# A chain of attention, a channel mix and a gated mix on one core: the value weight by seven products

## The chip, the cores and the metric

One core of a Trainium2 chip runs the whole program. The metric is the device time of one execution in microseconds; smaller is better. Engines: PE (TensorE, matmuls), DVE (VectorE), ACT (ScalarE), POOL (GpSimd), SP (SyncE, which here only issues DMAs).

## The reference

Three operations in a row, all in fp32, batch 8, 576 positions. An attention with random features (8 heads of 64) gives x of 512 channels. A first mix and a second mix follow, each batch by itself:

```python
# attention: phi(x) = [exp(p), exp(-p)], p = x @ w_phi less its largest magnitude
num = q_p @ (k_p.T @ v); den = q_p @ k_p.sum(seq) + 1e-6; x = num / den
# first mix, w_k 512x1024, w_v 1024x512, w_r 512x512
xk = mu_k * x + (1 - mu_k) * x_prev;  xr = mu_r * x + (1 - mu_r) * x_prev
x = sigmoid(xr @ w_r) * (relu(xk @ w_k) ** 2 @ w_v)
# second mix, w_val 512x512, conv_w 5x512, w_out 512x512
gate = sigmoid(causal convolution of x with conv_w)
out = (gate * (x @ w_val)) @ w_out
```

## The kernel before

A product of two fp32 matrices is made of three passes: each operand is split into a high half of reduced precision (ACT copies it) and the low rest (DVE subtracts), and high x high, high x low and low x high are added in a PSUM bank. Four of the five weight products (k, r, v, out) moreover go by seven products instead of eight, after Winograd: both matrices are cut into four quarters, seven sums of quarters are multiplied, and the results joined. The fifth, by the value weight, is plain: `gemm`, four column tiles by two halves by twelve matmuls of 128x128 by 128x288, 96 in a round; `split` makes its four high and four low halves in the page `y`.

The program runs in two parts. In the attention (up to some 297 us) PE projects, turns and sums, and beside it the weights are converted from the 64-bit input: `narrow` on ACT and DVE, sums of quarters (`combine`) and halves (`part_two`, `pool_tt`) on POOL and ACT, then to DRAM (`ws`); wk alone stays in SBUF (`wkt`). The second part has rounds `it` = 0 to 8. A round multiplies batch `it` by k (`st_k`), r (`st_r`) and v (`st_v`), and batch `it - 1` by value (`st_val`) and out (`st_out`); DVE and ACT run that batch's convolution (`conv`) beside it. On PE a round has three phases: k alone, then r and value by turns, then v and out by turns. Weight units of 1 MB are fetched by SP (`fetch_unit`) into a ring of three pages u0 to u2 or into a page that is free (xf, dd, ot).

`seven` drives r and out: `combos` yields sums of quarters one after the other, `operand` splits each into a place of the ring `ops`, which has four places for all products together. Results go from banks to SBUF through ACT copies and DVE additions; with `fork`, `begun` copies the first product's bank to a second one so that sums continue in it. Round `it`'s x lies in the page `xx`, loaded by `prep`, which mixes it with its shifted copy (ACT and DVE) into `xf` and `dd`.

The order on each engine is not the order of the code: every step is a task with a due time (`when`, in units of TIME us for a round; T, ODD and FIRST for the attention), and `Order.run` lays the tasks out on the engines by costs written in the file, each engine executing its list in order. Lines the prediction touches: L386 matmul, L960 ACT copies (`acts`), L402 the low halves (`less`), L951 sums (`dve`), L954 multiply-adds (`fma`), L420 loads, L486 and L497 POOL's sums and casts of conversion, L1066 the memset in `prep`, L1103 `begun`.

Of the kernel before, what the change touches and what calls it, by code (L numbers as in the profile page):

```python
# [20 lines left out]
TB = 288  # L21
# [4 lines left out]
def pattern(bits):  # L26
# [9 lines left out]
ODD = dict(q_proj=-0.118, k_proj=-0.204, turn=-0.103, sums=0.978, num=0.197, back=0.009)  # L36
FIRST = dict(q_proj=-5.403, k_proj=-0.991, tails=-2.94, turn=-1.923, sums=-0.992)
FROM, TO = 0, 28.375
# [6 lines left out]
PORT = 0.234  # L45
# [12 lines left out]
SOON, EARLY = 0, 0.332  # L58
SPLIT, FORK_R = 8, False
LIMIT = 1.274  # L60
# [252 lines left out]
def build(ctx, tc, qt, kt, vv, wphi, mu, wk, wr, wv, wval, cw, wout, out):  # L313
# [194 lines left out]
    def combine(quarters, n, emit):  # L508

        (a11, t11), (a12, t12), (a21, t21), (a22, t22) = quarters  # L510
        f = sb("F", [128, 512])
        s1 = (lambda: f[:, 0:n])
        pool_tt(n, s1, a21, a22, ALU.add, [t21, t22], [(f, 0)], new=[f])
        emit(0, a11, [t11])
        if n == 512:
            s3, t3 = a21, t21
            pool_tt(n, s3, a11, a21, ALU.subtract, [t11], [t21])
            s2, t2 = a11, t11
            pool_tt(n, s2, s1, a11, ALU.subtract, [(f, 0)], [t11])
# [11 lines left out]
        emit(6, a22, [t22])  # L531
# [3 lines left out]
    def convert(name, w, group, k, tick):  # L535
# [20 lines left out]
        elif name != "wk" and k == 1:  # L556
            stage = []

            def emit(p, x, r):
                if p % 2 == 0:  # L560
                    stage.append(sb("ql", [128, 2, 2, 256]))
                hl, e, u = stage[-1], p % 2, units[name] + (p if name == "wv" else p // 2)
                at = (lambda h: hl[:, e, h]) if name == "wv" else (lambda h: hl[:, h, e])
                part_two(x, lambda: at(0), lambda: at(1), 256, r, [(hl, e, h) for h in range(2)],
                         new=[] if e else [hl])
                if e or p == 6:
# [11 lines left out]
            combine([((lambda q=q, c=c: q[:, 256 * c:256 * c + 256]), (q, c)) for q, c in  # L578
                     ((got[0], 0), (got[1], 0), (got[0], 1), (got[1], 1))], 256, emit)
# [320 lines left out]
    def moe():  # L900
# [21 lines left out]
        TIME = 79.6  # L922
# [90 lines left out]
        def combos(ops, n, q, tmp, parts, due):  # L1013

            def sub(p, out, x, y):
                due(p, None)
                dve(n, out, x, y, ALU.subtract, tokens(x, y), out.tok)

            def op(p, k):
                for i, x in enumerate(parts(tmp if k is None else q[k])):  # L1020
                    due(p, i)
                    ops[p, i] = operand(x)

            op(0, 0)
            yield
            op(1, 2)
            sub(1.4, tmp, q[3], q[1])
            sub(1.6, q[1], q[1], q[0])
            sub(1.8, q[0], q[3], q[1])
            yield  # L1030
            for p, k in enumerate((0, 1, None, 3, 2), 2):
                op(p, k)
                if p == 2:
                    sub(2.2, q[2], q[2], q[0])
                yield
# [25 lines left out]
        def prep(it):  # L1061
# [3 lines left out]
            if it == 0:  # L1065
                add("POOL", 0.15, lambda: nc.gpsimd.memset(x()[:, :, 0:1], 0.0), r=[("page", "xx")], w=["x0"])  # L1066
# [18 lines left out]

        def split(it, t, c, x, dst):
            when(it, t)
            h, l = (At(dst or ("xx", "dd")[i], 2304 * i * bool(dst) + 576 * c, 576) for i in range(2))
            acts(576, lambda: h(F32R), x, AF.Copy, x.tok, h.tok)
            add("DVE", d_time(576), lambda: less(nc.vector, l(F32R), x(), h(F32R)), r=tokens(x, h), w=l.tok)  # L1090
# [62 lines left out]
        def st_v(it, start):  # L1153
# [7 lines left out]
            for p in range(7):  # L1161
# [3 lines left out]
                u = fetch_unit(it, start(p) - 10, units["wv"] + p, None if p else ("xf", 0))  # L1165
# [41 lines left out]
        def gemm(name, it, start, src, after):  # L1207

            mov = [At(src or ("xx", "dd")[i], 2304 * i * bool(src), 4, 2, 288) for i in range(2)]
            for m in range(4):  # L1210
                if m == 0:
                    when(it, start(0) - 10)
                    renew("xf", F32R)
                if m % 2 == 0:
                    u = fetch_unit(it, start(2 * m) - 10, units[name] + m // 2, None if m else ("xf", 0))
                o = wide()
                for h in range(2):
                    t = start(2 * m + h)
                    when(it, t)
                    add("PE", t_mm(TB, 12), lambda m=m, h=h, o=o, u=u: product(  # L1220
                        o, h, [(unit_at(u, 0, c, m % 2), unit_at(u, 1, c, m % 2)) for c in range(4)],
                        [[a(F32R)[:, c, h] for c in range(4)] for a in mov], True, True),
                        r=tokens(*mov) + u.tok, w=[o], new=[] if h else [o])
                when(it, t - SOONER)
                after(m, o, both(o), t + 1.6)

        def seven(name, it, start, q, tmp, p5, land, lead, places, fork):
# [3 lines left out]
                           lambda p, i: when(it, start(p) - lead if i is not None else start(0) + p - lead - 4))  # L1231
            banks = {}
            for p in range(7):
# [5 lines left out]
                if p == 6 or isinstance(place, tuple):  # L1239
# [4 lines left out]
                for _ in range(1 if p or 0 < it < 7 else 2):  # L1244
                    next(steps, None)
# [30 lines left out]
        def st_r(it, start):  # L1276
            land = {(a, h): x2_pair(it, 2 * a, h) for a in range(2) for h in range(2)}
            q = [At("dd", 576 * i, 2, 288) for i in range(4)]
            for got in seven("wr", it, start, q, At("tmp", 0, 2, 288), At("sp", 1152, 2, 288), land, 10, [None] * 6 + [("ot", 0)],
                             FORK_R and it > 0):  # L1280
                if got is None:
                    continue
                t, a, h, b, r = got
                when(it, t)
                x = land[a, h]
                acts(576, x, b or x, AF.Sigmoid, r, x.tok)
# [25 lines left out]
        def st_out(i, it, start):  # L1312
            land = {(a, h): At("y", 1152 + 1152 * a + 576 * h, 2, 288) for a in range(2) for h in range(2)}
            q = [x2_pair(i, 2 * a, h) for a in range(2) for h in range(2)]
            for got in seven("wout", it, start, q, At("y", 0, 2, 288), At("y", 576, 2, 288), land, 8,
                                       ["dd", ("dd", 1024), ("ot", 0), ("dd", 0), ("dd", 1024), ("ot", 0), None] if it < 7 else [None] * 7, it < 7):
# [12 lines left out]
        for it in range(9):  # L1329
# [3 lines left out]
            if it:  # L1333
                conv(it - 1, it, -10, 1.8)
                when(it, 6 if it < 8 else -30)
                if it == 8:
                    renew("xx", F32R)
                    renew("dd", F32R)
                else:
# [6 lines left out]
            if it < 8:  # L1346
                st_r(it, at(22.3, 3.18))
            if it:
                st_val(it, at(23.9, 3.18))
                if it < 8:  # L1350
                    when(it, 47)
                    renew("y", F32)
            v = st_v(it, at(46.2, 4.77 if 0 < it < 7 else 3.18)) if it < 8 else ()
            o = st_out(it - 1, it, at(49.4, 4.77) if it < 7 else at(68.5 if it == 7 else 49.4, 1.59)) if it else ()
# [109 lines left out]
```

## Time and profile before

| | before |
|---|---|
| median of 3 runs | 941.8 us (937.82 to 941.82) |
| the profiled execution | 946.79 us |
| its span, first to last instruction | 945.0 us |
| PE busy | 911.5 us, 96% |
| DVE, ACT busy | 822.9 us, 719.0 us |
| POOL busy (attention only) | 185.8 us |
| granted PE clock, mean | 0.994 |

The rows come from one profiled execution, so sums are made against its own 946.79 us (945.0 us of span and 1.8 us around it); the median of the runs is 5.0 us lower. Busy is the time in which at least one instruction of the engine is on record. Instructions of ACT and DVE overlap their neighbours a little, so the distance of two starts says what one costs when they follow each other.

### The profile page before, as it was taken

To read this page: it belongs to the slowest core of one execution; us is meant where nothing else is said; L and a number is where in the kernel's file an instruction comes from. 1 tells how busy PE (TensorE), PEld (TensorE's weight loads), DVE (VectorE), ACT (ScalarE), POOL (GpSimd) and SP (SyncE) were. 2 spreads that over 40 slices of the span, in tenths; PEclk is the share of its full clock that TensorE was granted. 3 is DMA by queue.
4 is the path that set the end of the run, shared out by engine and by line. 5 is a ranking of instruction groups with operands and counts; after the bars stand their busy time and mean duration, and the time that the engine had idled before them with its cause. 6 is when DMAs were issued, how large, how long until landed. Compare 5 with 4: busy or idle time off the path is not lost.

```text
span 945.0 us, 28048 instructions
## 1 busy us (share of the span) xinstructions
PE 911.5 (96%) x11696; PEld 895.0 (95%) x11696; DVE 822.9 (87%) x1276; ACT 719.0 (76%) x1435; POOL 185.8 (20%) x322
## 2 busy tenths in 40 slices
PE   7999989998998999999999999999999999999997
PEld 6998988898898999999999999999999999999997
DVE  5999989888877799789979978988997897899695
ACT  4998978888798979479767947966876794787453
POOL 0387975675671000000000000000000000000000
PEclk9999999999999999999999999999999999999999
DMA  6657788888866583777488477658738847764883
GB/s 218 206 196 221 234 265 291 285 264 285 287 223 218 206 283 121 254 271 244 167 298 288 151 268 273 229 223 277 269 113 301 291 154 282 252 196 172 281 308 133
DMA packets 79774, 224.33 MB, mean 237 GB/s; under 512 B 10144, under 2 KB 35104, under 8 KB 66592
## 3 DMA queue, kind: packets, MB, share of 16 engines
q1 hardware_dynamic: 70784, 213.04, 66.3%
q10 hardware_dynamic: 8864, 9.50, 2.8%
q8 instruction: 92, 1.51, 0.7%
q14 instruction: 34, 0.28, 0.1%
HBM read 186.87 MB, written 35.65 MB: 235 GB/s over the span
## 4 chain that ended last, share of the span: by engine, by line
PE 76%; DVE 8%; ACT 6%; DMA 4%; issue 3%; POOL 2%; ACTq 0%; SPq 0%; DVEq 0%; POOLq 0%
PE c L386 59%; PE b L386 15%; PE b L749 2%; DVE ops L402 2%; DMA out<-y 1%; DVE dd L662 1%; DVE x L951 1%; POOL wkt L486 1%; DMA ops<-in_kt 1%; DMA xx<-in_wr 1%; ACT u L718 1%; ACT ops L960 1%; DMA xx<-in_wval 1%; DMA u<-ws 1%; DMA xx<-in_wv 1%
## 5 line engine op out<-in xcount | busy, mean ns | idle before, releaser
L386 PE MATMUL c<-ops,u 128*128 128x288 f32 x1968 | 275.7, 296 | 5.0 <-DVE ops L402 3.4
L386 PEld LDWEIGHTS c<-ops,u 128*128 128x128 f32 x1968 | 266.3, 188 | 7.2 <-DVE ops L402 4.4
L386 PE MATMUL c<-ops,wkt 128*128 128x288 f32 x1344 | 180.2, 295 | 2.3 <-ACT x L399 1.2
L386 PEld LDWEIGHTS c<-ops,wkt 128*128 128x128 f32 x1344 | 178.3, 188 | 3.2 <-ACT x L399 1.3
L662 DVE TENSOR_REDUCE dd<-b 128x4 f32<-128x512 f32 (+1 forms) x144 | 86.5, 622 | 20.8 <-PE b L386 19.6
L954 DVE SCALAR_TENSOR_TENSOR g<-x,cwt,g 128x576 f32<-128x576 f32 x128 | 102.4, 819 | 0.0
L960 ACT ACTIVATE ops<-k 128x576 fp32r<-128x576 f32 x96 | 65.3, 681 | 46.4 <-PE c L386 43.8
L402 DVE TENSOR_TENSOR ops<-k,ops 128x576 fp32r<-128x576 f32 x96 | 71.8, 756 | 26.0 <-ACT ops L960 25.8
L386 PE MATMUL b<-wph,ops 64*128 64x128 f32 x1152 | 88.3, 288 | 6.3 <-DMA ops<-in_kt 4.4
L386 PEld LDWEIGHTS b<-wph,ops 64*128 64x128 f32 x1152 | 77.1, 194 | 9.7 <-ACT u L718 3.2
L386 PE MATMUL b<-g,y 128*64 128x65 f32 x2176 | 74.4, 224 | 5.3 <-issue 3.0
L386 PEld LDWEIGHTS b<-g,y 128*64 128x64 f32 x2176 | 68.9, 139 | 8.2 <-issue 3.6
L767 ACT ACTIVATE y<-b 128x512 f32<-128x512 f32 x128 | 68.5, 627 | 4.2 <-PE b L749 3.2
L960 ACT ACTIVATE sp<-c 128x576 f32<-128x576 f32 x50 | 32.5, 650 | 42.9 <-PE c L386 42.7
L960 ACT ACTIVATE k<-k 128x576 f32<-128x576 f32 x98 | 63.1, 681 | 0.3
L399 ACT ACTIVATE x<-b 128x260 f32<-128x260 f32 (+3 forms) x112 | 40.5, 416 | 11.0 <-PE b L749 5.2
L386 PE MATMUL c<-y,u 128*128 128x288 f32 x336 | 48.0, 294 | 0.0
L386 PE MATMUL c<-y,xf 128*128 128x288 f32 x336 | 46.8, 295 | 0.0
L386 PEld LDWEIGHTS c<-y,u 128*128 128x128 f32 x336 | 45.7, 188 | 0.0
L386 PEld LDWEIGHTS c<-y,xf 128*128 128x128 f32 x336 | 45.3, 188 | 0.0
L960 ACT ACTIVATE k<-c 128x576 f32<-128x576 f32 x64 | 41.3, 646 | 5.1 <-PE c L386 3.9
L960 ACT ACTIVATE ops<-xf 128x576 fp32r<-128x576 f32 x48 | 32.7, 683 | 13.8 <-PE c L386 7.9
(160 smaller groups left out, 1819.3 us busy)
## 6 DMA issues: line engine op xcount, KB each, us to landing
u<-ws SPq DMA_DIRECT2D x86, 1024.0 KB, 5.4
xf<-ws SPq DMA_DIRECT2D x16, 1024.0 KB, 6.0
ws<-dd SPq DMA_DIRECT2D x28, 512.0 KB, 4.8
dd<-ws SPq DMA_DIRECT2D x24, 512.0 KB, 5.8
ot<-ws SPq DMA_DIRECT2D x20, 512.0 KB, 5.7
xs<-x SPq DMA_DIRECT2D x16, 576.0 KB, 4.6
xx<-xs SPq DMA_DIRECT2D x8, 1152.0 KB, 7.5
out<-y ACTq DMA_DIRECT2D x32, 288.0 KB, 5.3
```

What stands on the lines that cost most here:

```text
L386: latest[0] = nc.tensor.matmul(**kw)
L399: act(out=out, in_=x, func=AF.Copy)
L402: eng.tensor_tensor(out=out, in0=x, in1=hi.bitcast(F32), op=ALU.subtract)
L486: nc.gpsimd.tensor_tensor(out=o[:, c], in0=a[:, c], in1=b[:, c], op=op)
L662: add("DVE", t_dve(128 * n), lambda: nc.vector.tensor_reduce(out=m[:, 0:n, 0], in_=b3[:, 0:n], axis=AX.X, op=ALU.max, apply_absolute_value ...
L718: act(out=e[:, c, half], in_=b3[:, c], func=AF.Exp, scale=-1.0 if half else 1.0, bias=m[:, 1 - half, c:c + 1])
L749: latest[0] = nc.tensor.transpose(out=out, in_=x[r], identity=ident[r, r])
L767: add("ACT", t_act(512), lambda y=y, half=half: act(out=e[:, y, half, :], in_=bs[y][:], func=AF.Exp, scale=-1.0 if half else 1.0), r=[bs[y ...
L951: add("DVE", d_time(n), lambda: tt(out=out(), in0=x(), in1=y(), op=op), r=r, w=w)
L954: add("DVE", d_time(n) + 0.06, lambda: stt(out=out(), in0=x(), scalar=scalar(), in1=y(), op0=ALU.mult, op1=ALU.add), r=r, w=w)
L960: act(out=out(), in_=x(), func=func, **more)
```

## The change

The value weight of rounds 1 to 7 goes by seven products as well: `st_val` calls `seven` with `fork`, and its products alternate with those of r, as those of v and out do. Sums of quarters are made from x in `x2` into the page `xx` (argument `into`), the operands go through the ring `ops`, and `split` into `y` disappears; `y` receives weight units. The gate (DVE) multiplies each joined quarter. Because `xx` is now used up to the end of value, x of the next round is loaded after that, and its zero column is set anew by a POOL memset in each round. The last round (`last_val`) multiplies plainly as before, from quarters a11, a12, a22 and a21, so a21 is stored as an eighth unit. The value weight's conversion makes sums of quarters like the others: four units per column group, `ws` grows from 34 to 38. The due times of the attention (T, ODD, FIRST, FROM) and some constants of the order are new; TIME is 78.0 instead of 79.6.

```diff
-T = dict(load_q=-5.614, load_k=-4.036, load_v=-2.112, tails=-1.806, q_proj=-1.855, k_proj=-1.864, turn=-0.024,
-         sums=-1.263, num=0.201, back=1.217, finish=1.434, convert=0.307, ones=-1.742, num_step=0.488, scale=0.715,
-         prep=-0.343)
...
+T = dict(load_q=-5.752, load_k=-3.673, load_v=-2.132, tails=-1.806, q_proj=-1.854, k_proj=-1.864, turn=-0.024,
+         sums=-1.263, num=0.201, back=1.217, finish=2.23, convert=0.226, ones=-2.034, num_step=0.361, scale=0.715,
+         prep=-0.396)
...
-FROM, TO = 0, 28.375
+FROM, TO = 0.892, 28.375
...
-    SEVEN = ("wr", "wout")
-    units = {"wr": 0, "wval": 4, "wv": 6, "wout": 13}
-    ws = dram.tile([128, 34, 4, 256], F32, name="ws")
+    SEVEN = ("wr", "wval", "wout")
+    units = {"wr": 0, "wval": 4, "wv": 8, "wout": 15}
+    ws = dram.tile([128, 38, 4, 256], F32, name="ws")
...
-    def combine(quarters, n, emit):
+    def combine(quarters, n, emit, whole=False):
         (a11, t11), (a12, t12), (a21, t21), (a22, t22) = quarters
+        if whole:
+            emit(6, a22, [t22])
+            emit(7, a21, [t21])
...
-        TIME = 79.6
+        TIME = 78.0
...
-        def combos(ops, n, q, tmp, parts, due):
+        def combos(ops, n, q, tmp, parts, due, into=None):
+            at = into or (q[1], q[0], q[2])
...
-            if it == 0:
-                add("POOL", 0.15, lambda: nc.gpsimd.memset(x()[:, :, 0:1], 0.0), r=[("page", "xx")], w=["x0"])
+            add("POOL", 0.15, lambda: nc.gpsimd.memset(x()[:, :, 0:1], 0.0), r=[("page", "xx")],
+                w=["x0"] + [k for c in range(4) for k in span("xx", 577 * c, 1)])
...
+                if isinstance(place, list):
+                    u = fetch_unit(it, start(p) - 10, units[name] + p // 2, place)
+                elif p == 6 or isinstance(place, tuple):
...
         def st_val(it, start):
-            def after(m, o, b, t):
-                g, y = At("g", 576 * m, 576), x2_at(it - 1, m, 0, 576)
-                dve(576, lambda: halves(y()), lambda: halves(g()), b, ALU.mult, [o] + g.tok, y.tok)
-
-            gemm("wval", it, start, "y" if it < 8 else None, after)
+            t = [At("xx", 576 * i, 2, 288) for i in range(4)]
+            land = {(0, 0): None, (0, 1): t[2], (1, 1): t[0]}
+            q = [x2_pair(it - 1, 2 * a, h) for a in range(2) for h in range(2)]
+            places, late = [["y", 0], 0, ["y", 2048], 0, None, 0, ("y", 0)], []
+
+            def gated(d, a, h, b, r):
+                when(it, d)
+                g, x, y = Two("g", 1152 * a, 576, TB * h), q[2 * a + h], land.get((a, h))
+                dve(576, x, b or y, g, ALU.mult, (r or y.tok) + g.tok, x.tok)
+
+            for p, got in enumerate(seven("wval", it, start, q, t[0], t[1], land, 10, places, True, 1,
+                                          (t[1], t[2], t[3]))):
+                for x in late:
+                    gated(*x)
...
-                for c in range(4):
-                    split(it, (SPLIT if it < 8 else -24) + 2 * c, c, x2_at(it - 1, c, 0, 576), "y" if it < 8 else None)
...
-                st_r(it, at(22.3, 3.18))
+            rs = st_r(it, at(22.3, 3.18)) if it < 8 else ()
+            vs = () if not it else st_val(it, at(23.9, 3.18)) if it < 8 else last_val(it, at(*END[2:4]))
+            if 0 < it < 8:
+                for _ in zip(rs, vs):
+                    pass
...
-            v = st_v(it, at(46.2, 4.77 if 0 < it < 7 else 3.18)) if it < 8 else ()
+            v = st_v(it, at(44.6, 4.77 if 0 < it < 7 else 3.18)) if it < 8 else ()
```

## Rows read from the trace of the kernel before

**Rows 1.** The page: engines' busy time and share; chain that ended last, by engine.
```profile
PE 911.5 (96%) x11696; PEld 895.0 (95%) x11696; DVE 822.9 (87%) x1276; ACT 719.0 (76%) x1435; POOL 185.8 (20%) x322
PE 76%; DVE 8%; ACT 6%; DMA 4%; issue 3%; POOL 2%; ACTq 0%; SPq 0%; DVEq 0%; POOLq 0%
```

**Rows 2.** Busy time by stretches of 80 us (start:end length, busy us, instructions).
```profile
core 0: us, PE busy (x) PEld busy (x) DVE busy (x) ACT busy (x) POOL busy (x), PEclk, DMA share, GB/s
352.00:432.00 80.00, 78.83 (x591) 78.36 (x590) 70.19 (x98) 58.17 (x97) 0.00 (x0) 1.00 0.64 218
...
512.00:592.00 80.00, 80.00 (x605) 80.00 (x604) 71.26 (x100) 59.54 (x99) 0.00 (x0) 1.00 0.68 243
```

**Rows 3.** The same by phases of round 3: k; r, value; v, out.
```profile
512.70:535.00 22.30, 22.30 (x170) 22.30 (x170) 22.30 (x33) 21.73 (x38) 0.00 (x0) 1.00 0.63 225
535.00:559.00 24.00, 24.00 (x183) 24.00 (x182) 19.21 (x26) 13.69 (x23) 0.00 (x0) 1.00 0.62 230
559.00:592.50 33.50, 33.50 (x253) 33.50 (x252) 29.55 (x42) 23.92 (x39) 0.00 (x0) 1.00 0.76 264
```

**Rows 4.** PE in order of time: start, length, what, count (neighbours merged).
```profile
460.76 4.92 PE L386 MATMUL c<-y,xf 128*128 128x288 f32 x36
...
471.10 1.76 PE L386 MATMUL c<-ops,u 128*128 128x288 f32 x12
472.69 1.76 PE L386 MATMUL c<-y,u 128*128 128x288 f32 x12
...
540.48 1.74 PE L386 MATMUL c<-y,xf 128*128 128x288 f32 x12
```

**Rows 5.** DVE in order of time, in a k phase.
```profile
689.92 0.75 DVE L402 TENSOR_TENSOR y<-x,y 128x576 fp32r<-128x576 f32 x1
690.59 0.75 DVE L402 TENSOR_TENSOR ops<-dd,ops 128x576 fp32r<-128x576 f32 x1
```

**Rows 6.** DVE in v and out; in brackets idle before, and its releaser.
```profile
652.82 0.76 DVE L402 TENSOR_TENSOR ops<-x,ops 128x576 fp32r<-128x576 f32 x1 [0.72 <-ACT ops L960]
654.42 0.76 DVE L402 TENSOR_TENSOR ops<-tmp,ops 128x576 fp32r<-128x576 f32 x1 [0.84 <-ACT ops L960]
```

**Rows 7.** ACT in order of time.
```profile
538.62 0.68 ACT L960 ACTIVATE ops<-tmp 128x576 fp32r<-128x576 f32 x1
539.20 0.68 ACT L960 ACTIVATE k<-k 128x576 f32<-128x576 f32 x1
```

**Rows 8.** Page's DMA issues (us to landing); then in time memset, issue, mixing, operand.
```profile
xx<-xs SPq DMA_DIRECT2D x8, 1152.0 KB, 7.5
...
275.00 0.11 POOL L1066 MEMSET xx<- 128x4 f32 x1
...
517.76 0.37 SPq L420 DMA_DIRECT2D xx<-xs  x1
...
563.31 0.77 ACT L960 ACTIVATE xf<-xx,mut 128x576 f32<-128x576 f32 x1
...
588.92 0.76 DVE L402 TENSOR_TENSOR ops<-xf,ops 128x576 fp32r<-128x576 f32 x1
```

**Rows 9.** Busy time by stretches of the attention, columns as in rows 2.
```profile
90.00:120.00 30.00, 27.75 (x732) 26.32 (x732) 29.16 (x54) 28.38 (x80) 29.34 (x44) 1.00 0.73 229
210.00:240.00 30.00, 26.90 (x638) 25.08 (x637) 27.18 (x54) 24.00 (x66) 19.86 (x32) 0.94 0.87 284
```

**Rows 10.** Instructions of L486 and L450: ns shortest/median/longest, first and last start.
```profile
L486 POOL TENSOR_TENSOR dd<-xf,dd x41: 717/730/1250, 112.3 to 279.5; 128x256 fp32r<-128x256 f32 x41
...
L450 DVE SCALAR_TENSOR_TENSOR xf<-xx,xf x18: 652/685/1200, 30.9 to 265.4; 128x512 int32<-128x512 int32 x18
```

**Rows 11.** Groups by line and shape: POOL's casts (busy us, mean ns, idle before).
```profile
L497 POOL CAST dd<-ot 128x256 fp32r<-128x256 f32 x6 | 2.4, 394 | 0.1
```

**Rows 12.** Who waited for whom in attention, PE: us in total, times, longest.
```profile
PE b L386 <- issue: 5.9, 5, 2.3
```

**Rows 13.** Busy time by stretches of 4 us, columns as in rows 2.
```profile
200.00:204.00 4.00, 4.00 (x40) 3.60 (x40) 2.84 (x8) 3.09 (x11) 1.97 (x3) 0.57 0.89 250
```

More of the change, by code (lines that the diff above doesn't have):

```diff
@@ L530, in combine @@
         emit(5, a12, [t12])
-        emit(6, a22, [t22])
+        if not whole:
+            emit(6, a22, [t22])
     ready = {}
@@ L1084, in prep @@
                     fma(576, out, was, lambda r=r, c=c: omm[:, r, c:c + 1], out, x.tok + ["x0", "omm"], toks)
[L1086 to L1090, printed above, removed]
         def square(it, t, x):
@@ L1164, in st_v @@
                     renew("xf", F32R)
-                u = fetch_unit(it, start(p) - 10, units["wv"] + p, None if p else ("xf", 0))
+                if it == 7 and p == 1:
+                    when(it, start(0) - 9)
+                    renew("dd", F32R)
+                u = fetch_unit(it, start(p) - 10, units["wv"] + p,
+                               ("dd", 0) if it == 7 and p == 1 else None if p else ("xf", 0))
                 fresh = p in FRESH and not (fork and p == 1)
@@ L1205, in st_v, with seven @@
                 yield
[L1207 to L1227, printed above, removed]
+        def seven(name, it, start, q, tmp, p5, land, lead, places, fork, ahead, into=None):
             ops = {}
             steps = combos(ops, 576, q, tmp, lambda x: [x],
-                           lambda p, i: when(it, start(p) - lead if i is not None else start(0) + p - lead - 4))
+                           lambda p, i: when(it, start(p) - lead if i is not None else start(0) + p - lead - 4), into)
             banks = {}
@@ L1243, in seven @@
                 fresh = p in FRESH and not (fork and p == 1)
-                for _ in range(1 if p or 0 < it < 7 else 2):
+                for _ in range(1 if p else ahead):
                     next(steps, None)
@@ L1279, in st_r @@
             for got in seven("wr", it, start, q, At("tmp", 0, 2, 288), At("sp", 1152, 2, 288), land, 10, [None] * 6 + [("ot", 0)],
[L1280 to L1286, printed above, removed]
+                             FORK_R and it > 0, 1 if it else 2):
+                if got is not None:
+                    t, a, h, b, r = got
+                    when(it, t)
+                    x = land[a, h]
+                    acts(576, x, b or x, AF.Sigmoid, r, x.tok)
+                yield
         def conv(i, it, t0, step):
@@ L1301, in conv, with split @@
                 acts(576, g, g, AF.Sigmoid, [], g.tok)
-        def st_val(it, start):
-            def after(m, o, b, t):
-                g, y = At("g", 576 * m, 576), x2_at(it - 1, m, 0, 576)
-                dve(576, lambda: halves(y()), lambda: halves(g()), b, ALU.mult, [o] + g.tok, y.tok)
-            gemm("wval", it, start, "y" if it < 8 else None, after)
+        def split(it, t, c):
+            when(it, t)
+            x, (h, l) = At("x2", 2432 * (it - 1 & 1) + 608 * c + 32, 576), (At(p, 576 * c, 576) for p in ("xx", "dd"))
+            acts(576, lambda: h(F32R), x, AF.Copy, x.tok, h.tok)
+            add("DVE", d_time(576), lambda: less(nc.vector, l(F32R), x(), h(F32R)), r=tokens(x, h), w=l.tok)
@@ new lines, in last_val @@
+        def last_val(it, start):
+            when(it, -30)
+            renew("xx", F32R)
+            renew("dd", F32R)
+            for c in range(4):
+                split(it, -24 + 2 * c, c)
+            mov = [At(p, 0, 4, 2, 288) for p in ("xx", "dd")]
+            for m in range(4):
+                j = m // 2
+                if m % 2 == 0:
+                    u = fetch_unit(it, start(2 * m) - 10, units["wval"] + 3 * j, None if m else ("xf", 0))
+                o, g, x = wide(), At("g", 576 * m, 576), At("x2", 2432 * (it - 1 & 1) + 608 * m + 32, 576)
+                at = [2 * (i if j == 0 else 1 - i) + c for i in range(2) for c in range(2)]
+                for h in range(2):
+                    t = start(2 * m + h)
+                    when(it, t)
+                    add("PE", t_mm(TB, 12), lambda m=m, h=h, o=o, u=u, at=at: product(
+                        o, h, [(unit_at(u, 0, k, m % 2), unit_at(u, 1, k, m % 2)) for k in at],
+                        [[a(F32R)[:, c, h] for c in range(4)] for a in mov], True, True),
+                        r=tokens(*mov) + u.tok, w=[o], new=[] if h else [o])
+                when(it, t + 1.6)
+                dve(576, lambda x=x: halves(x()), lambda g=g: halves(g()), both(o), ALU.mult, [o] + g.tok, x.tok)
+                yield
@@ new lines, in st_val @@
+        def st_val(it, start):
+            t = [At("xx", 576 * i, 2, 288) for i in range(4)]
[10 more added lines that the diff above has]
+                    gated(*x)
+                late = []
+                if got and p == 4:
+                    late.append(got)
+                elif got:
+                    gated(*got)
+                yield
```

56 lines of the change are left out of this document (27 added, 29 removed).

## Prediction, before the change was run

> **What bounds the kernel now.** I read the page first: PE is busy for 96% of the span, DVE for 87%, ACT for 76%, and the chain that ended last lies on PE for 76% [rows 1]. An average says little here, so I cut the span in two. Up to 297 us the attention runs; from there to the end come nine rounds of the second part. The table by 80 us stretches shows what a round is like: in each of the four middle stretches (one row of them is shown, DVE differs by 0.1 us among them) PE is busy 80.00 of 80.00 us at a granted clock of 1.00, DVE 71.2 us, ACT 59.5 us and POOL not at all [rows 2]. So from round 2 to round 5 nothing but the number of matmuls sets the time, and DVE has 8.8 us of idle time in a stretch to give away. The same table cut by phases shows where this lies: in the k phase (22.3 us) DVE is full, in the phase of r and value it is busy 19.21 of 24.0 us, in the phase of v and out 29.55 of 33.5 us [rows 3]. The third view is PE in order of time: the value weight's first product starts at 460.76 us in one round and at 540.48 us in the next, a round of 79.72 us [rows 4].
>
> **Matmuls taken away.** By the code a round has 168 matmuls of k, 84 of r, 96 of value, 168 of v and 84 of out: 600, so 79.72 / 600 = 0.1329 us each. The operand's place doesn't matter: twelve from ops take 1.59 us until twelve from y start, which is 12 x 0.1325 [rows 4]. Seven products of twelve are 84 instead of 96. It happens in rounds 1 to 7, the last round stays plain: 7 x 12 x 0.1329 = 11.2 us less on PE. This part lies whole on the path.
>
> **DVE work added.** Plain value takes four subtractions for the low halves and four gating multiplications. Seven products take seven low halves, four sums of quarters, two additions that join products, and four gates: 17 instead of 8, nine more. Back to back such an instruction comes every 0.67 us (starts 689.92 and 690.59), though its row says 0.75 [rows 5]. So 9 x 0.67 = 6.0 us in a round, and DVE goes from 71.0 (71.2 x 79.72 / 80 [rows 2]) to 77.0 us busy while the round on PE shrinks to 588 x 0.1329 = 78.1 us. The slack falls from 8.7 to 1.1 us. This is the weak place of the change.
>
> Phase by phase: the k phase loses the four low halves of y that stand in it today [rows 5] and gets the four sums of quarters in their place, so it stays full, as it is today without PE waiting. The r and value phase becomes 22.4 us long and gets seven low halves and two additions: 19.2 + 6.0 = 25.2 us, 2.8 us more than it holds. The phase of v and out has 4.0 us idle, and its gaps are of one kind: in round 4 there are six, 3.8 us together, five of them waits for an ACT copy into ops (two are shown, 0.72 and 0.84 us) and one for a copy out of a bank [rows 6]. DVE had run out of things to do. 2.8 us of lag fits there. An operand has four places in the ring ops, so it can be made some three products (4.8 us) ahead of its use; a lag of 2.8 us stays below that. The rate of one operand in 1.6 us is what v and out already run at, with no PE idle. So I cost DVE at nearly nothing, with that slack as cover. The bounds: nothing a round (the k phase today, DVE full and PE full [rows 3]), to 2.9 us a round, if as much idle time stays on DVE as v and out leave today (77.0 + 4.0 - 78.1). I take 0.2 us a round, 1.4 us in all, near the k phase's row since most of a round will look like it; the first stretch, where PE lost 1.2 us today [rows 2], is part of my reason not to take zero.
>
> **ACT work added.** Three more copies into ops, one copy that forks a bank and three copies out of banks: 7 x about 0.58 us (their spacing when back to back [rows 7]) = 4.1 us, from 59.4 to 63.5 of 78.1. The r and value phase, where ACT is busy 13.69 of 24 us [rows 3], has room. Cost: nothing; if that cover went, an operand would come 0.6 us later, inside the ring's lead.
>
> **The x load and the new memset.** Temporary sums now live in xx, so the next round's x can't be loaded during the k phase (517.76 us today) but only when the fifth value product's gate has read xx, by the phase lengths some 23 us into the r and value phase. POOL's memset comes first (0.11 us in the one it does today), then SP's issue, behind which the weight fetches of v and out queue, and 7.5 us to land [rows 8]. So the mixing on ACT starts some 10 us into the phase of v and out instead of 4.3 us (563.31 against 559). Its result is needed by the first operand from xf at 588.92 us, 29.9 us into that phase [rows 8], so some ten us of cover are left, and the mix moves into the very time in which DVE has gaps. Cost nothing; if SP stood at this load for 2 us, the fetch behind it would be 2 us late, with the ring u refilled one unit ahead of use. A round also fetches 1.5 MB more into y; DMA is busy 0.62 in that phase [rows 3]. Nothing.
>
> **Attention.** Value's conversion gets combinations and eight units instead of a plain split: 24 POOL subtractions and sums instead of 8, eight casts of 256 instead of two of 512, which I count as four of 256: 16 x 0.73 [rows 10] + 4 x 0.39 [rows 11] = 13.2 us more on POOL, as many casts more on ACT, and 2 MB more written to ws. The times of everything in attention are set anew besides, which no row can show. POOL is busy 19.9 of 30 us in a stretch where value is converted now, but 29.3 of 30 in an earlier one [rows 9]. Bounds: POOL carries 2% of the chain [rows 1], 18.9 us of its 185.8 us busy, a tenth; a tenth of 13.2 is 1.3 us. At worst each of the 16 additional sums holds up a DVE instruction by what separates the middle from the longest of L450's rows, 1.20 - 0.685 = 0.5 us [rows 10]: 8 us, all on the chain. At best the new order is better: PE's L386 waits 5.9 us for "issue" in attention [rows 12], and over 4 us its granted clock was 0.57, near the lower of its two levels, 1.2 and 2.4 GHz, which is 1.7 us lost [rows 13]; half of both is 4 us. From -4 to +8, taken +1.3.
>
> The Trainium skill ("SBUF — State Buffer", section "Who interferes with whom") says that a VectorE instruction with two SBUF inputs and a GpSimd one that reads SBUF exclude each other for their whole length. The rows agree in part: L450 reaches 1.20 us, yet its median of 0.685 us says that most don't meet POOL. By the rule in full attention's term would be nearer to +8 and the whole time to 940 us, by the medians it stays near +1.3.
>
> **Sum.** -11.2 + 1.4 + 1.3 = -8.5 us. The profiled execution took 946.79 us with a span of 945.0, 5 us over the median of 941.8; matmul counts save the same in both, so I take it off the median: 941.8 - 8.5 = 933.3 us.
>
> **Rivals.** First, attention eats most of the gain: POOL is full in 90 to 120 us [rows 9], the conversions are denser (planned weights of 165.2 instead of 151.2, begun later, finished at the same place) and push it, and the +8 end is reached: 941.8 - 11.2 + 1.4 + 8 = 940.0 us. For it speaks the full POOL row; against it, that POOL has a third of its time free where the new work falls due.
>
> Second, slower: DVE becomes the bound in the rounds. It executes in order, so a low half that PE needs stands behind gates, convolution steps and sums; with 77.0 us of work, PE keeps its gain only if DVE's idle time stays under 1.1 us a round, and from 79.72 - 77.0 = 2.7 us idle a round the kernel loses. If the 4.0 us that v and out leave today stay, a round is 81.0 us: 7 x 1.3 = +9, with attention's 1.3, 952 us. For it: DVE's idle time there is waits for ACT, not lack of order, and such waits may stay. Against it: 2.8 us of late work will be at hand in that phase, and the k phase shows DVE full over 22 us without a PE wait [rows 3]. At half of it (2.0 us idle) a round is 79.0 us, 7 x 0.7 = 5 us are saved, and with attention's 1.3 it is 938 us.
>
> The Trainium skill ("TensorE: Matmul & The Clock Gate", table at the head) calls VectorE's queue strictly first in, first out, eight deep; the waits of [rows 6] agree, and it is what would make this rival bite.
>
> Third, the change saves nothing on PE, because the seven products stall on their banks: r and value would then hold four pairs of banks, as v and out do today without a wait. I give it little; the 11.2 us would come back as waits, and attention's 1.3 us remain: 943 us.
>
> **How the numbers follow.** My forecast (929 to 937 us) gets 0.56, attention better than forecast (under 929) 0.06, the first rival and DVE's half way (937 to 944) 0.22, the third 0.03, the slower rival 0.13. About 0.5%, 4.7 us, is what a measurement can tell from no change. Below 937.1 lie the forecast, the better case and a part of the half way: 0.65; within 0.5% 0.23; above 946.5 us 0.12. The range goes from the lower edge of the better case to the upper edge of the first rival: 928 to 944 us.
>
> **What would show it.** Right: 84 matmuls of value a round, value starts 78.1 to 78.4 us apart, DVE over 76.5 us busy a round, and first matmul of the second part at 297 to 300 us. Wrong in DVE's step: PE waits named "DVE ops L402" or "DVE x" inside the rounds. Wrong in the step of xx: PE waits behind an operand from xf at the head of the k phase. Wrong in attention: that first matmul later than 303 us or before 294 us.

## The result, and the profile after

The changed kernel takes 932.76 us (median of 8 runs, 930.57 to 936.7) against 941.81 us for the kernel before in the same comparison: a ratio of 0.9908, 95% interval 0.9887 to 0.993. That is 9.05 us less; forecast were 8.5 us less and 933.3 us. The profiled execution has a span of 930.2 us and took 932.31 us.

The page of the changed kernel: busy time by engine (to be read against [rows 1]), its chain by engine, and the landing of the x load (against [rows 8]).

```profile
PE 899.3 (97%) x11612; PEld 882.8 (95%) x11612; DVE 860.2 (92%) x1339; ACT 749.3 (81%) x1490; POOL 205.2 (22%) x351
PE 87%; ACT 5%; DVE 4%; DMA 2%; issue 2%; POOL 0%; SPq 0%; DVEq 0%; ACTq 0%; POOLq 0%
...
xx<-xs SPq DMA_DIRECT2D x8, 1152.0 KB, 9.1
```

84 matmuls are gone (11,696 to 11,612), PE is busy 12.2 us less, and DVE 37.3 us more. PE carries more of the chain than before: nothing has taken its place.

PE in order of time, changed kernel: the k group of each round, with start, length and count of matmuls; in brackets the idle time before it and what ended it.

```profile
294.88 19.56 PE L387 MATMUL c<-ops,wkt 128*128 128x288 f32 x144 [1.20 <-ACT x L400]
...
352.77 19.31 PE L387 MATMUL c<-ops,wkt 128*128 128x288 f32 x144 [0.54 <-ACT c L1104]
...
427.91 22.38 PE L387 MATMUL c<-ops,wkt 128*128 128x288 f32 x168
...
506.21 22.38 PE L387 MATMUL c<-ops,wkt 128*128 128x288 f32 x168
...
584.50 22.38 PE L387 MATMUL c<-ops,wkt 128*128 128x288 f32 x168
...
819.39 22.38 PE L387 MATMUL c<-ops,wkt 128*128 128x288 f32 x168
```

The same view of the kernel before, which shows how its rounds went:

```profile
297.50 19.56 PE L386 MATMUL c<-ops,wkt 128*128 128x288 f32 x144 [1.21 <-ACT x L399]
...
355.44 19.31 PE L386 MATMUL c<-ops,wkt 128*128 128x288 f32 x144 [0.59 <-ACT c L1103]
...
432.95 22.38 PE L386 MATMUL c<-ops,wkt 128*128 128x288 f32 x168
...
752.06 22.38 PE L386 MATMUL c<-ops,wkt 128*128 128x288 f32 x168
...
832.97 22.38 PE L386 MATMUL c<-ops,wkt 128*128 128x288 f32 x168
```

A round went from 79.72 us [rows 4] to 78.30 us, five times the same. The spans differ by 945.0 - 930.2 = 14.8 us, and the two lists say where: the attention ends 2.6 us earlier (294.88 against 297.50), round 1 is 2.4 us shorter (75.14 against 77.51), the five middle rounds 8.5 us (391.48 against 400.02), and the rest to the end 1.2 us (110.81 against 112.03). The middle rounds hold 5 x 1.42 = 7.1 us that come in every round, and 1.4 us that belongs to this one execution of the kernel before: its round from 752.06 lasted 80.91 us, and two others were slightly long. Without that, the rounds give 2.4 + 7.1 + 1.2 = 10.7 us. The attention's 2.6 us are not the change's: further down single profiles of one attention differ by more.

Busy time by stretches, changed kernel, columns as in [rows 2]: a whole round, then the three phases of the next one, to be read against [rows 3].

```profile
506.20:584.50 78.30, 78.30 (x590) 78.25 (x589) 76.19 (x109) 63.41 (x105) 0.10 (x1) 1.00 0.75 266
584.50:606.70 22.20, 22.20 (x170) 22.20 (x169) 22.20 (x34) 19.02 (x33) 0.00 (x0) 1.00 0.73 265
606.70:629.20 22.50, 22.50 (x171) 22.44 (x170) 22.44 (x33) 19.93 (x34) 0.00 (x0) 1.00 0.57 188
629.20:662.80 33.60, 33.60 (x255) 33.60 (x254) 31.55 (x45) 24.45 (x39) 0.10 (x1) 1.00 0.89 317
```

PE is full in all three. DVE is now full in k and in r and value (22.44 of 22.50 us, before 19.21 of 24.0), and what doesn't fit there fills half of the idle time of v and out: 31.55 of 33.60 us, before 29.55 of 33.5. Of its 2.1 us of idle time in a round 2.05 lie in that last phase.

### The profile page after: what moved, and what is told of

Read it like the earlier page. It is cut to its first block, busy times and chain, and to the rows that moved or that the text cites. A ratio compares the mean times of both kernels' runs of the same rounds, so it can differ in the third digit from the quotient of the medians.

```text
span 930.2 us, 28059 instructions
## 1 busy us (share of the span) xinstructions
PE 899.3 (97%) x11612; PEld 882.8 (95%) x11612; DVE 860.2 (92%) x1339; ACT 749.3 (81%) x1490; POOL 205.2 (22%) x351
## 4 chain that ended last, share of the span: by engine, by line
PE 87%; ACT 5%; DVE 4%; DMA 2%; issue 2%; POOL 0%; SPq 0%; DVEq 0%; ACTq 0%; POOLq 0%
PE c L387 64%; PE b L387 21%; PE b L755 2%; DMA ops<-in_kt 1%; DVE ops L403 1%; ACT y L773 1%; ACT u L724 1%; DMA xx<-in_wk 1%; ACT ops L966 1%; ACT x L400 1%; DVE dd L668 0%; DVE x L957 0%; DVE xf L960 0%; DVE sp L670 0%; ACT xf L966 0%
## 5 line engine op out<-in xcount | busy, mean ns | idle before, releaser
L387 PE MATMUL c<-ops,u 128*128 128x288 f32 x2112 | 295.9, 296 | 3.6 <-DVE ops L403 1.9
L387 PEld LDWEIGHTS c<-ops,u 128*128 128x128 f32 x2112 | 286.0, 188 | 5.5 <-DVE ops L403 2.3
L387 PE MATMUL b<-wph,ops 64*128 64x128 f32 x1152 | 85.8, 284 | 8.3 <-DMA ops<-in_kt 4.9
L387 PEld LDWEIGHTS b<-wph,ops 64*128 64x128 f32 x1152 | 74.8, 190 | 11.9 <-ACT u L724 3.6
L966 ACT ACTIVATE ops<-x 128x576 fp32r<-128x576 f32 x69 | 46.9, 680 | 18.7 <-PE c L387 12.7
L387 PE MATMUL c<-ops,y 128*128 128x288 f32 x420 | 61.6, 295 | 0.0
L387 PEld LDWEIGHTS c<-ops,y 128*128 128x128 f32 x420 | 57.9, 188 | 0.0
L403 DVE TENSOR_TENSOR ops<-x,ops 128x576 fp32r<-128x576 f32 x69 | 51.7, 750 | 3.0 <-ACT ops L966 3.0
```

The lines of the kernel that those rows point to most:

```text
L387: latest[0] = nc.tensor.matmul(**kw)
L403: eng.tensor_tensor(out=out, in0=x, in1=hi.bitcast(F32), op=ALU.subtract)
L966: act(out=out(), in_=x(), func=func, **more)
```

## The experiments

They ran in three groups, each beside fresh runs of the kernel before (medians 940.58, 939.9 and 939.36 us). Theory one is that of the prediction: matmuls give the gain, DVE has just enough room, attention costs little. The rivals are those of the prediction, and as a further one, that the new due times of the attention bring the gain.

**The change again** (`after_again`), to have it beside the others on one chip.

> The changed kernel as it is, for a second profile. If the gain lies in the rounds, every round from 2 to 6 is 78.3 us again and the second part (first k product of 144 to the end) some 635 us as in the first profile; only the attention's end (294.9 us in the first) may differ, by some 3 us. If the rounds' time were itself scattered, round lengths would differ between the two profiles.

Measured: 932.46 us, ratio 0.9912 (0.9882 to 0.9942). All rounds took 78.30 us. The k group after the attention starts at 296.13 us in this profile, 1.2 us later than in the first one, from the same program.

**The change with the due times of before** (`old_times`).

```diff
-T = dict(load_q=-5.752, load_k=-3.673, ...
-FROM, TO = 0.892, 28.375
+T = dict(load_q=-5.614, load_k=-4.036, ...
+FROM, TO = 0, 28.375
```

> The changed kernel with the attention's due times and cost constants of the kernel before. Theory (the gain is matmuls in the rounds, attention is a wash): 932 to 935 us, rounds still 78.3 us. Rival (the new order is what pays for the heavier conversion): attention ends some 4 us later, 936 to 940 us.

**The kernel before with the new due times** (`new_times`): the same constants the other way round.

> The kernel before with only the attention's new due times and constants; conversion and products stay as they were. Theory (attention is a wash): 940 to 944 us, rounds 79.7 us. Rival (the new order by itself is faster): 936 to 939 us.

Measured: `old_times` 935.39 us, ratio 0.994 (0.9919 to 0.996), `new_times` 947.43 us, ratio 1.0068 (1.0047 to 1.0089). Due times alone bring no gain; on the old conversion they lose 0.5 to 0.9%. With the change they go along with 2.9 us (935.39 against 932.46), but the two intervals overlap, so this is not shown. The gain, then, isn't that of the new order by itself; whatever it is worth, it is worth only with the work it was made for.

**The conversion alone** (`conv_only`): kernel before, new due times, the value weight converted as for seven products and then multiplied plainly.

```diff
-    SEVEN = ("wr", "wout")
+    SEVEN = ("wr", "wval", "wout")
...
-                        o, h, [(unit_at(u, 0, c, m % 2), unit_at(u, 1, c, m % 2)) for c in range(4)],
+                        o, h, [(unit_at(u, 0, c, m % 2), unit_at(u, 1, c, m % 2)) for c in at],
```

> The kernel before with the new due times and with the value weight converted as for seven products, but multiplied plainly in every round. Theory: the conversion costs 1.3 us over the previous kernel (POOL has room), 941 to 945 us; the rounds stay 79.7 us. Rival (POOL's additional sums hold DVE up): 946 to 950 us, attention's end 4 to 8 us later.

Measured: 943.17 us, ratio 1.0019 (1.0002 to 1.0037): new attention without the new products costs 2.6 us by the medians. The products are then worth 943.17 - 932.46 = 10.7 us. The lists of k groups gave 10.7 us without the lengthened rounds that are described next, and some 11.9 with them; medians of so few runs don't tell the two apart.

PE in order of time, `conv_only`, in its first middle round:

```profile
428.75 22.38 PE L386 MATMUL c<-ops,wkt 128*128 128x288 f32 x168
...
454.23 4.13 PE L386 MATMUL c<-ops,u 128*128 128x288 f32 x29 [1.37 <-DVE ops L402]
...
510.11 22.38 PE L386 MATMUL c<-ops,wkt 128*128 128x288 f32 x168
```

ACT in the same round:

```profile
440.97 1.26 ACT L965 ACTIVATE y<-x 128x576 fp32r<-128x576 f32 x2 [1.84 <-DMA out<-y]
```

This round lasted 81.36 us, the others of this execution 79.72 to 79.99, as the kernel before has one of 80.91 at 752.06 us. Of the 25 middle rounds in the five profiles of kernels with plain value (before, `new_times`, `conv_only`, `pool16`, `store2`) nine are over 0.1 us longer than 79.72, by 0.14 to 1.64 us, 6.2 us together; of the 20 in `after`, `after_again`, `old_times` and `dve2_vout` none differs from 78.30 by 0.05 us. In the kernel before the one from 752.06 us can be followed. First the step in its chain of waits, then ACT, then PE in order of time:

```profile
753.91 9.76 DMA out<-y
```

```profile
763.83 1.26 ACT L960 ACTIVATE y<-x 128x576 fp32r<-128x576 f32 x2 [1.39 <-DMA out<-y]
```

```profile
777.10 3.06 PE L386 MATMUL c<-ops,u 128*128 128x288 f32 x21 [0.93 <-DVE ops L402]
```

A store of the output out of `y` took 9.76 us, the plain value's high halves had to wait for it to be gone from `y`, DVE fell behind, and PE stood 13 us later. The same holds of all nine: in each of them ACT waits 0.35 to 1.84 us for this store, which is issued 1.9 us into the k phase, and in the other 16 rounds it waits at most 0.26 us. In the 25 rounds the store took 7.4 to 10.2 us, over 8.7 in the nine. With seven products no halves are written into `y`; its next writer is a weight load, which started 9.2 to 11.6 us into the k phase without a wait of PE. So these rounds went with the change, and they had cost some 6.2 / 5 = 1.2 us an execution.

**DVE work added in k, r and value** (`dve2`, `dve4`, `dve8`): value's sums of quarters are made anew; two of the four twice (1.3 us of DVE work a round more), all four twice (2.7 us), all four three times (5.4 us).

```diff
-                dve(n, out, x, y, ALU.subtract, tokens(x, y), out.tok)
+                for _ in range(1 + (1 if into and p > 1.7 else 0)):
+                    dve(n, out, x, y, ALU.subtract, tokens(x, y), out.tok)
```

> The changed kernel with two of value's sums of quarters made twice in rounds 1 to 7 (2 x 0.67 = 1.3 us more DVE work a round, same values). DVE's idle time in a round is 78.3 - 76.2 = 2.1 us. Theory (DVE stays covered while its work fits): rounds 78.3 us, total as the changed kernel. Rival (the idle time can't be used because it is waits): rounds 79 to 79.6 us, 5 to 9 us more.

> All four of value's sums of quarters made twice (2.7 us more DVE work a round, same values). Theory: 76.2 + 2.7 = 78.9 us of DVE work no longer fit in 78.3, rounds 78.9 to 79.3 us, 4 to 7 us more in all. Rival (DVE's order has slack that busy time doesn't show): rounds 78.3 us.

> Each of value's four sums of quarters made three times (5.4 us more DVE work a round, same values). Theory: 81.6 us of DVE work set the round, 81.6 to 82.5 us, 23 to 29 us more in all. Rival: under 80 us.

Measured: 941.38, 948.5 and, from two runs, 969.98 us (ratios 1.0024, 0.9984 to 1.0063; 1.0067, 1.0038 to 1.0097; 1.0297, 1.0209 to 1.0384, all against the kernel before). Rounds of 79.70, 80.88 and some 83.6 us, so 1.40, 2.58 and 5.3 us more than 78.30: the added work is paid in full, already at the least addition that was tried.

Busy time by phases of a round, `dve2`, columns as before:

```profile
590.93:613.15 22.22, 22.22 (x171) 22.22 (x170) 22.22 (x34) 19.01 (x33) 0.00 (x0) 1.00 0.71 259
613.15:636.70 23.55, 23.38 (x174) 22.91 (x173) 23.38 (x33) 20.45 (x35) 0.00 (x0) 1.00 0.56 203
636.70:670.61 33.91, 33.39 (x251) 33.15 (x250) 31.91 (x46) 24.11 (x39) 0.10 (x1) 1.00 0.84 299
```

and two stalls of PE in that round, with one each of `dve4` and `dve8`:

```profile
618.66 0.93 PE L387 MATMUL c<-ops,u 128*128 128x288 f32 x5 [0.15 <-DVE ops L403]
...
645.04 2.53 PE L387 MATMUL c<-ops,u 128*128 128x288 f32 x17 [0.52 <-DVE ops L403]
```

```profile
617.43 1.73 PE L387 MATMUL c<-ops,y 128*128 128x288 f32 x11 [0.90 <-DVE ops L403]
```

```profile
626.54 1.73 PE L387 MATMUL c<-ops,y 128*128 128x288 f32 x11 [2.90 <-DVE ops L403]
```

DVE still has 2.0 us of idle time in v and out, as without the added work, while PE waits for low halves in r and value and once more 8 us into v and out (645.04 us). DVE's first gap of over 0.2 us there begins at 652.5 us, after that wait. Idle time that comes later didn't serve the work ahead of it. The row of PE shows 0.17 + 0.52 us of the loss, that of the weight loads (PEld) 23.55 - 22.91 = 0.64 and 33.91 - 33.15 = 0.76 us, together the whole 1.40.

**The same DVE work in v and out** (`dve2_vout`): k's first sum of quarters, which DVE makes during v and out of the round before, made three times for the k of rounds 2 to 7.

```diff
-                dve(n, out, x, y, ALU.subtract, tokens(x, y), out.tok)
+                for _ in range(3 if p == 1.4 and again else 1):
+                    dve(n, out, x, y, ALU.subtract, tokens(x, y), out.tok)
```

> The changed kernel with k's first sum of quarters (tmp from xf) made three times in rounds 1 to 6: 2 x 0.67 = 1.3 us more DVE work a round as in dve2, same values, but placed in the phase of v and out, where DVE has 2.05 us idle, instead of ahead of the phase of r and value. Theory by phases (only k with r and value is full on DVE): rounds stay at 78.3 to 78.5 us. Rival (DVE's work of the whole round is the bound): 79.6 to 79.7 us as in dve2.

Measured: 931.08 us, ratio 0.9907 (0.9877 to 0.9937), rounds of 78.30 us: free. The phase of v and out in this kernel:

```profile
629.60:663.17 33.57, 33.57 (x253) 33.57 (x253) 32.61 (x47) 24.46 (x39) 0.10 (x1) 1.00 0.89 317
```

DVE took in 1.06 us more there (32.61 against 31.55) with PE full. The same 1.3 us of work costs 1.40 us a round in one phase and nothing in the other.

**PE made lighter** (`pe_light`): value's third pass is left out in rounds 1 to 7, 28 matmuls a round, which is 3.7 us.

```diff
-                for a, b in ((wh, 0), (wh, 1), (wl, 0)):
+                for a, b in ((wh, 0), (wh, 1), (wl, 0))[:2 if two else 3]:
```

> The changed kernel without the third pass (low half of the weight times high half of x) in value's products of rounds 1 to 7, so the values lose precision: 28 matmuls fewer, PE work 78.3 - 28 x 0.133 = 74.6 us a round. Theory (DVE is next, 76.2 us of work): the round falls only to 76.2 to 76.8 us, 10 to 15 us less in all. Rival (DVE isn't near the bound): 74.6 us, 26 us less.

Measured, from two runs: 922.78 us, ratio 0.9796 (0.9716 to 0.9876). The round, and one of PE's waits in the next:

```profile
577.97:655.30 77.33, 75.94 (x562) 74.64 (x561) 75.98 (x109) 62.77 (x105) 0.10 (x1) 1.00 0.75 269
```

```profile
622.52 1.72 PE L387 MATMUL c<-ops,xf 128*128 128x288 f32 x11 [0.55 <-DVE ops L403]
```

Of 3.7 us a round only 0.97 came (78.30 to 77.33). The rest is idle time on PE, 1.39 us by its own row and 77.33 - 74.64 = 2.69 us by that of the weight loads; all its waits of over 0.15 us in these rounds are for low halves or sums of DVE. The next microsecond of this kernel is DVE's: rival two stands just behind the change and would have come with any more work in these phases.

**The x load twice** (`x_twice`), to put a later x to the test: the second load has to wait for the first.

```diff
-            load(lambda: x()[:, :, 1:577], lambda: xs[it].rearrange("c d s -> d c s"), 1179648,
+            for _ in range(2):
+                load(lambda: x()[:, :, 1:577], lambda: xs[it].rearrange("c d s -> d c s"), 1179648,
```

> The changed kernel loading x into xx twice in every round (same values, 1.15 MB more, x is there some 4 us later). Theory (ten us of cover between the mixing and the first operand that needs it): rounds 78.3 to 78.6 us. Rival (the late load is already close to the path): PE waits at the head of k, rounds above 80 us.

Measured: 947.77 us, ratio 1.0096 (1.0064 to 1.0127), rounds of 80.8 us. Queue of SP, ACT and DVE in order of time, in the changed kernel and, second, in `x_twice`:

```profile
629.48 0.37 SPq L421 DMA_DIRECT2D xx<-xs  x1
...
641.32 1.43 ACT L966 ACTIVATE xf<-xx,mut 128x576 f32<-128x576 f32 x2
...
647.74 0.75 DVE L957 TENSOR_TENSOR tmp<-xf 128x576 f32<-128x576 f32 x1
...
659.33 0.75 DVE L403 TENSOR_TENSOR ops<-xf,ops 128x576 fp32r<-128x576 f32 x1
```

```profile
639.36 0.36 SPq L421 DMA_DIRECT2D xx<-xs  x1
...
646.10 1.15 SPq L421 DMA_DIRECT2D xx<-xs  x1
...
652.83 0.76 DVE L403 TENSOR_TENSOR ops<-x,ops 128x576 fp32r<-128x576 f32 x1 [0.89 <-PE c L387]
...
657.19 1.43 ACT L966 ACTIVATE xf<-xx,mut 128x576 f32<-128x576 f32 x2
657.32 0.76 DVE L403 TENSOR_TENSOR ops<-y,ops 128x576 fp32r<-128x576 f32 x1 [1.38 <-ACT ops L966]
...
666.67 0.75 DVE L957 TENSOR_TENSOR tmp<-xf 128x576 f32<-128x576 f32 x1
...
670.74 0.75 DVE L403 TENSOR_TENSOR ops<-xf,ops 128x576 fp32r<-128x576 f32 x1
```

The first fence covers one round, the second the same round of `x_twice`, which begins 6.58 us later in its trace (591.08 against 584.50). So its mix comes 657.19 - 641.32 - 6.58 = 9.3 us later and the operand 670.74 - 659.33 - 6.58 = 4.8 us later. The operand is still in time for the k phase at 671.86 us. But DVE stands idle before the mix (the two gaps shown, and 0.93, 0.53 and 0.30 us: 4.0 us between 650 and 658 us) and then has mixing, sums and halves from 658 us on into the next k phase, with one gap of 0.32 us up to 676 us. Its busy time in the round is the same as after the change (76.23 against 76.19 us), the round 2.5 us longer. It is much like the finding of `dve2`: work moved to a later place on DVE leaves idle time that isn't made good. PE's waits, 0.2 to 0.5 us at a time by the list, come later and are of two kinds: for low halves of DVE (4.1 us in the middle rounds) and for ACT's copies that start a second bank (2.0 us), the first of these 5 us into the k phase. No wait of PE is for a transfer; but what the second transfer does beside delaying the mix was not separated.

**More work in the old attention** (`pool16`, `store2`): in the kernel before, value's low halves are made three times on POOL (16 sums more, 11.7 us), or value's four stores to `ws` are issued twice (2 MB more).

```diff
+            for _ in range(2):
+                pool_tt(512, lambda: as_r(hl[:, :, 1]), ...
```

```diff
+            for _ in range(2):
                 load(lambda: ws[:, 2 * u:2 * u + 4, group], ...
```

> The kernel before, with the low halves of the value weight made three times in its conversion: 16 more POOL sums of 0.73 us (11.7 us), as many as the change adds; same values. If POOL's added work is what the heavier conversion costs at the old due times (5.5 us by old_times, conv_only and the kernel before), the total rises by 4 to 7 us. If POOL's work lies beside the path (a tenth of it on the chain), by 0 to 2 us.

> The kernel before, with each of the value weight's four stores to DRAM issued twice: 2 MB more written in the attention, as the change adds; same values. If the added traffic is what the heavier conversion costs, the total rises by 3 to 6 us, with more waits of PE for issue; if not, by 0 to 1 us.

Measured: 948.01 us, ratio 1.0078 (1.0053 to 1.0103), and 943.76 us, ratio 1.0037 (1.0016 to 1.0059). Either addition alone costs 3 to 9 us, and so does `new_times`, which adds no work at all; `conv_only` adds both kinds of work and costs some 2 us. So the price of a piece of conversion can't be told from that of a disturbed order. Which resource carries it stays open.

## Why the prediction was right, point by point

**Matmuls taken away, -11.2 us.** Right in place, and nearly in size. The rounds gave 10.7 us in the profiles, and the lengthened rounds that are gone add 1.2 us that the sum didn't have. By parts it is less regular: a middle round gave 1.42 us instead of 1.6 (last point), and round 1 gave 2.37 instead of 1.6. Of the 1.17 us that PE lost in the first stretch [rows 2], a wait of 0.6 us for a low half from DVE is gone; the one for an ACT copy (0.59 and 0.54 us in the lists) is left.

**DVE, +1.4 us.** Right within its bounds, the reasoning half right. The overflow from r and value into v and out came as worked out: 2.0 us more busy time there against 2.8 forecast, no PE wait that the view lists, and a round's DVE time of 76.2 us against 77.0, so that the mark of over 76.5 us was missed. What was wrong is the measure: the prediction weighed the slack of the round (8.7 to 1.1 us) and let rival two decide at 2.7 us of idle time a round. `dve2` shows a round with 2.0 us of DVE idle time that loses 1.40 us, `dve2_vout` one that loses nothing with the same work. What counts is how late DVE is at the low halves of r and value; there the margin was used up. In the changed kernel, in order of time, a group of PE, a low half of r on DVE, and PE's next group:

```profile
609.92 2.65 PE L387 MATMUL c<-ops,u 128*128 128x288 f32 x18
610.82 0.75 DVE L403 TENSOR_TENSOR ops<-dd,ops 128x576 fp32r<-128x576 f32 x1
612.40 1.76 PE L387 MATMUL c<-ops,y 128*128 128x288 f32 x12
```

The low half is ready at 611.57 us, and r's next product, the last six of the 18 matmuls, would begin at 609.92 + 12 x 0.1333 = 611.52 us. The 18 take 612.40 - 609.92 = 2.48 us, 0.08 more than 18 x 0.1333. So PE waits here already, too briefly for the view to name it, and the group takes 2.48 us in the round before as well. Over rounds 2 to 7 that is an estimated 0.5 us, which is what DVE cost in place of the 1.4 us taken.

The prediction called a lag of 2.8 us safe because operands can be made 4.8 us ahead. They can be, but after a full k phase they weren't. That this term came out small was luck: nothing more was asked of DVE, and there was no room for it. The Trainium skill ("TensorE: Matmul & The Clock Gate", table at the head) has VectorE as a strict first-in-first-out queue; `dve2` and `dve2_vout` agree, as 1.3 us of work a round costs 1.40 us or nothing by its place in the order.

**ACT, nothing.** Right: 63.41 us busy of 78.30 (forecast 63.5), and no wait of PE for ACT in the middle rounds.

**The x load, nothing.** Right in the result: the mix starts at 641.32 us, 12.1 us into v and out (forecast some ten), and PE doesn't wait. The cover was misjudged: ten us were counted to the first operand from `xf`, but DVE's sum from `xf` follows 0.6 us behind the last mixing instruction, and the work that the mix sets free has its place among DVE's last gaps of the round. `x_twice` has a mix 9.3 us later, which by the prediction's cover of some ten us should cost little, and pays 2.5 us a round.

**Attention, +1.3 us.** Right within its bounds. By medians it is +2.6 us (`conv_only`); by subtraction, the 11.9 us of the rounds less the 9.05 of the result, 2.9 us. So it was taken at half of what it cost, and the rounds gave some 2 us more than the sum had for them (11.9 against 11.2 - 1.4): that the total was met to 0.5 us is in part luck. Its mechanism isn't shown. POOL became 19.4 us busier instead of 13.2. The count was nearly right, for with the old due times the same instructions add 14.0 us (`old_times`, 199.8 us busy); with the new ones they take longer. The rows that the bound of 8 us was read from (every additional POOL sum holding up DVE) don't bear it out: L451, the former L450 of [rows 10], hardly changed, and neither did L450 in `pool16`, whose 16 additional sums cost 8.65 us by the medians.

```profile
L451 DVE SCALAR_TENSOR_TENSOR xf<-xx,xf x17: 640/693/1247, 33.1 to 262.7; 128x512 int32<-128x512 int32 x17
```

```profile
L450 DVE SCALAR_TENSOR_TENSOR xf<-xx,xf x18: 654/682/1268, 32.4 to 261.3; 128x512 int32<-128x512 int32 x18
```

The first is of the changed kernel, the second of `pool16`. Their medians are 693 and 682 ns beside 685 before, the longest 1,247 and 1,268 beside 1,200. So more work there can cost some 8 us, as `pool16` shows, but these rows don't show it to come this way. The exclusion that the Trainium skill states ("SBUF — State Buffer", section "Who interferes with whom") would in full have brought attention near +8; as before, most of these instructions meet no POOL sum that holds them up, and only the longest could be such a meeting.

The mark set for it, a first matmul between 297 and 300 us, was missed (294.88 us) without meaning anything: the same group starts at 296.13 in `after_again`, 295.24 in `dve2_vout`, 297.22 in `dve2` and 291.40 in `pe_light`, whose attention has the same tasks and due times. Single profiles scatter here by 5.8 us, more than the term that was to be read from them. Part of it may be the clock: over the first 285 us the mean granted clock, near the upper of its two levels in all, was 1.00 in the earliest of the five (`pe_light`), 0.98 in the latest (`dve2`) and in the kernel before, and 0.99 in the other three. Whether the lower clock or a wait of PE came first was not followed. The mark should have been one of medians.

**Rivals.** Attention eating the gain: `new_times` and `pool16` show that 6 to 9 us were possible. DVE as the bound: its edge is where the change ends, with 0.08 us of waiting a round and every addition ahead of the low halves paid (`dve2`). Stalls on banks: none seen, PE is busy 78.30 of 78.30 us.

**Why a middle round saves 1.42 us and not 12 x 0.1329 = 1.6.** The largest part is the 0.08 us for which PE waits at the low half of r. For the next, PE in order of time, a group of plain value in the kernel before with the one that follows, and two groups of the changed kernel:

```profile
540.48 4.92 PE L386 MATMUL c<-y,xf 128*128 128x288 f32 x36
545.24 0.96 PE L386 MATMUL c<-ops,u 128*128 128x288 f32 x6
```

```profile
606.72 1.76 PE L387 MATMUL c<-ops,u 128*128 128x288 f32 x12
608.32 1.76 PE L387 MATMUL c<-ops,y 128*128 128x288 f32 x12
```

Plain value's matmuls come every (545.24 - 540.48) / 36 = 0.1322 us here and every 0.1325 over all 96 of the round; those of r and value in the changed kernel come every (608.32 - 606.72) / 12 = 0.1333 us, as r's did before. Over value's 84 matmuls that is some 0.07 us; the prediction's 0.1329 was the mean of a round. Why the two differ by 0.0008 us stays open.

## What to carry to other kernels

Where an engine works in order, look for its slack in the phase that gets the work, and at how long before its use each result is ready; idle time elsewhere in the period is no cover. Matmul counts times a measured pitch predicted the gain of a round with a full PE to within 0.2 us (1.6 for 1.42), and no single profile of a stage that scatters by more than a term can confirm that term: use medians of a kernel with that part alone. A hand-made order belongs to its work: changing one without the other cost 0.7% (`new_times`) by the medians, and 0.3% within overlapping intervals (`old_times` beside the change).

## What the runs showed of the hardware that was not expected

- The scatter of one store can lengthen a round: of the 288 KB stores (median 5.3 us in the kernel before) those issued 1.9 us into a k phase took 7.4 to 10.2 us, and where the next writer of the source page had to wait 0.35 us or more for one, the round was 0.14 to 1.64 us longer.
- The x load, 1,152 KB, took 9.1 us (median) where the DMA share was 0.89, and 7.5 us before, when it was issued in a k phase of share 0.63.
- PE's busy row can hide short waits: in the round of `dve2` it lacks 0.69 us of a loss of 1.40, the row of the weight loads (PEld) lacks all of it.
- Work added to an engine that the page calls 92% busy was charged one for one (1.40, 2.58 and 5.3 us a round for 1.3, 2.7 and 5.4 us of work) where it lay in the phases in which that engine is full, and 1.3 us of it nothing in the phase where it is not.
